# Gated attention and long convolution: the convolution added after the last matmuls, and two of four table groups without their last addition

## The chip, the cores and the metric

The kernel runs on one core of a Trainium2 chip. The metric is the device time of one execution in microseconds, from its first to its last instruction with what lies around them. The core has four engines that compute here: TensorE (PE, matmuls into the PSUM banks; "PEld" is its weight loading), VectorE (DVE), ScalarE (ACT) and GpSimd (POOL, nearly unused). SyncE (SP) issues all DMAs. Each works through its own list of instructions in order and waits on semaphores.

## The reference, cut to what matters

Input x has 2048 tokens of 512 channels. Two branches read it, and a gate for each token mixes them.

```python
g = sigmoid((x * gate_w).sum(-1, keepdims=True))
# a: attention of 32 heads of 16, in 4 segments of 512 tokens, with a compressive memory
for s in range(4):
    p = softmax(qs @ ks.T * 0.25 + causal_mask)
    a_dot = p @ vs
    a_mem = (phi(qs) @ M) / (phi(qs) @ z + 1e-6)
    o = gh * a_mem + (1 - gh) * a_dot
    M, z = M + phi(ks).T @ vs, z + phi(ks).sum()
a = concat(o) @ wo
# b: one causal convolution over 2048 tokens for each channel
K = real(sum_n C[d,n] * exp(dt[d] * A[d,n] * l) * dt[d] * B[d,n])
b = irfft(rfft(K, 4096) * rfft(x, 4096))[:2048] + x * Dskip
out = g * a + (1 - g) * b
```

Everything is stored as bf16, and the output is bf16 as well.

## The kernel before, in words

A small scheduler class records operations (`op`, `evac`, `dma`) with what they read and write. The string `ORDER` (line 366) then lists every operation by its number: the order on each engine, SP's DMA queue included, follows from it. A trailing `a` or `v` says whether ACT or DVE does an operation that either can do (evacuations and copies, `evac`, line 224; such an operation shows up as line 226 or 229 on ACT and 227 or 230 on DVE). The numbers behind a slash are the buffers or PSUM banks. `replay` and `emit` turn that into five instruction lists with semaphore waits. Nearly every matmul goes through the helper in line 683.

The stages, interleaved by that order:

- *Preparation* (`ssm_prep`, `ssm_powers`, `ssm_cb`, lines 738 to 845): decay factors and their repeated squares, on ACT and DVE.
- *Attention* (`project`, `seg_tokens`, `seg_state`, `scores`, `ophase`), for 4 segments times 4 groups of 8 heads. `scores` makes five score tiles for each, 80 in all. Each tile fills the same four PSUM banks, and ACT takes its exponential (line 1063, 128x2048), so a score tile can be computed only when the exponential before it has been taken. Products of probabilities and values follow, then a normalisation on DVE (lines 1035 to 1038), and a transpose of the head outputs (`ophase`).
- *Tables* (`tables(c)`, lines 1131 to 1215), for 4 groups `c` of 128 channels. The convolution kernel K at lag l is a sum over 128 states. The lags are written as sums of an exponent in `F_EXP` (20) and one in `G_EXP` (32). DVE fills a table F and a table G of complex powers, doubling them: `cmul` (line 1149) multiplies entries by a power of the decay in three instructions, a product with one part (line 1159, into the table), a product with the other part (line 1162, into a buffer t2), and their addition (line 1166). G's entries 16 to 23 and 24 to 31 are two calls of eight entries each, instructions of 128x2048. There is one F and one G buffer and there are two t2 buffers.
- *Table sums* in the same function: for each of 32 positions four matmuls of 64 weight columns by 40 columns, in pairs on the left and right half of the columns, accumulate over real and imaginary parts. Four positions are one operation. The results are evacuated and sent by DMA into the tile KTT, which the transform stage reads.
- *Transforms* (`x_level1`, `tail`, lines 851 and 1219): a transform of x through DRAM (`scr_Z`), and, for two channel halves "a" and "b" of 16 steps each, matmuls, a product on DVE, matmuls back, and a last stage (`fir`). The convolution goes to DRAM (`scr_C`, four stores for each half) and is loaded again into four tiles CTT by segment, eight loads on SP, each waiting for the four stores of its half.
- *Final* (`final(s, tb)`, line 1309), for 16 blocks of 128 tokens: a PSUM bank gets an identity matmul of the convolution (512 columns), four matmuls of x with the diagonal skip (128 columns each) and four of the attention output with wo (512 columns each). ACT or DVE scales the result by 1-g (the attention output already carries g/(1-g)) and SP sends it out. In segment 3 the last of the four matmuls is an operation of its own, since the last heads' output comes late.

Of the kernel before, what the change touches and what calls it, by code (L numbers as in the profile page):

```python
# [348 lines left out]
def c_pe(mode, *ns):  # L349
    return ("P", mode, ns)  # L350
# [17 lines left out]
1225/0 1243/0/0 1231/3/1 1233/5 27a 1/0 34/13 32/4 33/9 17/0 35 36 37 46/11 15/0 1241/1 38/5 174/0 41/4 179/7 12/0 59v/0  # L368
45/13 13/4 47/0 49/1 23/0 57a 201/2/1/1 48 19/0 42 60/3 1244a 62/2 43 44 51/6 61 63v/4 72/2 75v/5 74/6 21/0 73 50/4 54/0
64 202a 84/2 1234a 86/1 18 16 85 87v/2 76 193/0 203 99v/6 52/13 96/2 204/0/0 1242a 589/0 98/2 378/0 97 100 53 28/4/0  # L370
211/7 29a 175/2 108/3 109/1 65 101 205a 294/5/0/2 110 176/0 122/5 77 123v/3 295a 209/1 111v/0 3/0 1232a 180/0 197/4
251/2/2/0 1246/1 213/3 215/0/0/1 120/2 121 88 252a 256/2/1/0 177/1 210a 1245/0 89 212a 1235 182/2 590/1 198/0 178 135v/8
257 591 220/0/1 800/0 221 132/1 66/3 134/6 136 199/0 990v/0 253 258 214v 67/2 133 207/1 222 989v 144/3 137 68 254/2/1
216 112 113 259 208v 2/0 218 145/1 146 5/0 993v/0 159v/7 158/3 997 992v 241/0/3 255a 998/0 242 160 991v 200/0 999
1257/2/1 994 243 1259/1 1260a 80/0 1258a 229/0/2 230 124 78/1 338/1/2 156/3 1247/2/0 1249/3 231 995/1 157 224/0/0 1003
225 339a 379/1 217 161 1261 996 1007/0 1004/1 147v/9 1005 79 219/0/0 380 1000 1248a 223/1 1001/1 1006 125 801/2 1250a
148 1226/3/1 1002 802 226 168v/1 1010/1 237/0/1 238 90/1 1009 91/5 227 1228/2 1008 1227a 239 1251 228 297/3/0 298a 382/0
1011 169 272/0/0 592 170 273 92 296 1262/3/0 1012 232 233/1 1229a 1230 149 236/2 240 244 245 1015 274 1263a 234 263/0/2
264 246/0 260 1013/1 247 102/1 1264/3 235/1 265 1016/0 104/6 1265a 248 103 114/1 267/0/1 268 1266 381 266/1 1014 261/0
1252/2/1 1017 1254/3 1021 269 1236/0/0 115/7 280/0/2 281 1255a 270 271 1238/3 275 1018 1253a 282 116 1019/0 126/1 1020  # L380
1024 276/4 277 1237a 1028/1 1027 249/2 250a/0 278/1 1267/1 1029 284/0/3 285 286 335/0/1/0 593 1025/0 803 987/0 336a
308/0/1 1256 309 279/0 1026 1239a 283 287 1283/1/1 1031/1 1285/2 310 1030 4/0 1286a 288 289/2 304/0/3 1284a 1022/0 305
384/1/2/1 290 1032 340/2/1/1 306 385a 1023 321/0/2 322 1287 341 1037/1/0 1041/3 1038 128/1 1039 1042 127 342 1033/2 323
140/3 1034 1035 313/0/0 1040a 1043a 343 291 314 183 307/1 311 312 386 1050v/0 1036a 315 1052v/0 1049v 1288/0 1048v 1056
196 1057/1 1051v 1275/2/1 1058 117v/4 337 138/1 1240 1062 1046/0 69v/6 1063/1 1273/3 1274a 1276a 325/0/3 326 327 316
1054/0 1289/2/0 317/0 1053 1064 387/3/0 388a 1055 347/0/1 318 1069/1 348 395/0/0 1059 1290a 319/0 1065 299/1/0/0 1066/0
139 349 1067 1074 320/2 324 1277 1045 328 1075/0 300 1291/3 356/0/2 70 129v/5 1292a 329 302 152/4 330/1 331 392 357 396a
1299/0/1 1301/3 81v/7 358 130 1068 1076 301 105v/0 1300a 150/3 1302a 332 351/0/3 352 399/0 292/3 444/1/1 353 93v/3 82
1293 445a 368/0/0 151 1060/0 1077 369 1280/1/0 1070 350/2 354 400a 355 1303 293a 359 1268/0/1 131 370 1278/3 1281a 1279a
106 364/0/1 165v/2 1078/1 1079 365 366 1061 1071 1269a 1270/3 1271a 71 1086 393/1 83 406/0/3 407 1282 1087/0 363/0 367  # L390
1044 166 1088 1272 408 360/3 448/0 361 1072/1 362/1 1296/2/0 394a 333/3 1073 94 334a 95 371 372 373/4 410/0/0 167 411
1047 1080 1090/0 1297a 1294/1 1089 153v/8 397/2 141v/1 374 412 423/0/2 1091 375 154 424 1081/0 1304/3/1 398a 303/0 344
1295a 107 409/1 1306/2 118 1083 425 1298 427/0/3 428 1307a 1305a 1308 164/5 413 1322/0 1084/1 376/2 441/3/1/0 429 345
442a 415/0/1 1085 119 1082 155 416 1100/3/0 1101 1092/0 1093 377a 1094 1309/1 262 443 1096/2 1097 1098 414 391/1 142
162/2 163 383/0 181 417 346 171v/9 1107v/0 1099a 1310/0 1311/2 473/0/0 474 1111v/0 1110v 1113/0 1109v 1108v 1115 422/2
426 418 1116/1 1095a 1102a 1112 419/0 1114 1324/0 1117 542/3/2 420 430 431 1323/1 475 1105 1104 543a 1325/0/2 1326a 1118
# [232 lines left out]

# [794 lines left out]
```

## Time and profile before

| | us |
|---|---|
| median of 3 runs | 312.86 |
| lowest and highest | 312.16, 313.46 |
| the profiled execution, whole | 313.44 |
| the profiled execution, span | 311.6 |
| PE busy | 267.4 |
| DVE busy | 262.9 |
| ACT busy | 270.0 |
| mean granted TensorE clock | 0.965 of full speed |

Busy time is time in which at least one instruction of the engine runs. Matmuls overlap one another, and so do neighbouring instructions on DVE and ACT a little; a mean duration in a row is therefore longer than the step from one to the next. In a row of the timeline stand the start and the time covered, the engine, the line, what it writes and reads, how many instructions are merged, and in brackets the idle time before with what ended it. A row of stretches has, for each engine, busy us and in brackets the number of instructions that touch the stretch, and then the granted clock, the DMA engines' share and GB/s.

### The profile page before, as it was taken

The numbers are of one execution on the slowest core, as the hardware profiler recorded it, in microseconds if no ns is written. First come the engines' busy times: TensorE is split into PE (matmuls) and PEld (weight loads), VectorE is DVE, ScalarE is ACT, GpSimd is POOL, SyncE is SP. The second block draws the span as 40 slices with busy tenths as digits, with TensorE's granted clock in tenths as the row PEclk, the third lists the DMA queues.
The fourth block names the chain that finished last, engine by engine and source line by source line (L and its number), as shares of the span: only waits on it lengthen the run. The fifth ranks groups of instructions, "written<-read, shape, count | busy, mean of one in ns | idle before, by whom it ended". The sixth has DMA issues, their size and how long they took to land.

```text
span 311.6 us, 9347 instructions
## 1 busy us (share of the span) xinstructions
PE 267.4 (86%) x3868; PEld 175.6 (56%) x3868; DVE 262.9 (84%) x638; ACT 270.0 (87%) x323; POOL 3.2 (1%) x9
## 2 busy tenths in 40 slices
PE   1787687698778899899988999999999999879991
PEld 1442354364444666586765576767767667555550
DVE  1999899989999989998999998989994999883440
ACT  2898998999999999989999989999899999985221
POOL 2000000000000000000000000000000000000000
PEclk9997995989998999999999999999999999998999
DMA  5999423151333754656665578787688784466141
GB/s 138 237 230 207 106 87 107 40 143 41 95 91 88 202 142 116 176 166 181 176 189 152 172 202 253 218 238 209 197 251 240 209 253 113 131 177 201 50 135 52
DMA packets 62362, 49.94 MB, mean 160 GB/s; under 512 B 23920, under 2 KB 57712, under 8 KB 62320
## 3 DMA queue, kind: packets, MB, share of 16 engines
q1 hardware_dynamic: 62320, 49.35, 56.7%
q8 instruction: 30, 0.49, 0.7%
q14 instruction: 12, 0.10, 0.1%
HBM read 29.02 MB, written 8.39 MB: 120 GB/s over the span
## 4 chain that ended last, share of the span: by engine, by line
PE 41%; ACT 35%; DVE 9%; DMA 7%; issue 4%; SPq 3%; DVEq 0%; ACTq 0%
PE psum L683 40%; ACT sb L1063 20%; ACT sb L226 12%; SPq L222 3%; DMA sb<-sb 2%; DVE sb L227 1%; DMA sb<-scr_Z 1%; DMA scr_C<-sb 1%; ACT sb L799 1%; DMA sb<-c_ident 1%; ACT sb L941 1%; DVE sb L1271 1%; ACT sb L992 1%; DMA sb<-c_negm 1%; DVE sb L1162 1%
## 5 line engine op out<-in xcount | busy, mean ns | idle before, releaser
L683 PE MATMUL psum<-sb 128*128 128x17 bf16 (+11 forms) x3780 | 261.2, 235 | 30.2 <-ACT sb L1063 17.6
L683 PEld LDWEIGHTS psum<-sb 128*128 128x128 bf16 (+3 forms) x3780 | 168.8, 99 | 119.3 <-ACT sb L1063 33.9
L1063 ACT ACTIVATE sb<-psum 128x2048 bf16<-128x2048 f32 x80 | 152.1, 1901 | 6.6 <-PE psum L683 6.4
L226 ACT ACTIVATE sb<-psum 128x512 bf16<-128x512 f32 (+3 forms) x171 | 100.3, 647 | 7.2 <-PE psum L683 6.4
L227 DVE CAST sb<-psum 128x512 bf16<-128x512 f32 (+1 forms) x52 | 35.3, 692 | 11.7 <-PE psum L683 10.0
L1159 DVE TENSOR_TENSOR sb<-sb 128x512 bf16<-128x512 bf16 (+3 forms) x52 | 34.0, 659 | 0.1
L1166 DVE TENSOR_TENSOR sb<-sb 128x512 bf16<-128x512 bf16 (+3 forms) x52 | 33.8, 661 | 0.1
L1162 DVE TENSOR_TENSOR sb<-sb 128x512 bf16<-128x512 bf16 (+3 forms) x52 | 33.7, 659 | 0.1
L1271 DVE TENSOR_TENSOR sb<-sb 128x1024 bf16<-128x1024 bf16 x32 | 21.8, 682 | 2.4 <-ACT sb L226 1.3
L1075 DVE TENSOR_TENSOR sb<-sb 128x1024 bf16<-128x1024 bf16 (+1 forms) x40 | 22.7, 576 | 1.0 <-ACT sb L1063 0.9
L229 ACT ACTIVATE sb<-psum,sb 128x512 bf16<-128x512 f32 x8 | 5.4, 686 | 14.9 <-PE psum L683 14.9
L1038 DVE TENSOR_TENSOR sb<-psum,sb 128x256 bf16<-128x256 f32 x32 | 13.3, 418 | 0.3
L230 DVE TENSOR_SCALAR sb<-psum,sb 128x512 bf16<-128x512 f32 x8 | 5.9, 747 | 6.9 <-PE psum L683 6.9
L1035 DVE RECIPROCAL sb<-psum 128x16 f32<-128x16 f32 x32 | 8.0, 251 | 4.2 <-PE psum L683 4.2
L799 ACT ACTIVATE sb<-sb 128x512 f32<-128x512 f32 x18 | 11.3, 643 | 0.0
L1115 DVE TENSOR_TENSOR sb<-psum,sb 128x512 bf16<-128x512 f32 x12 | 8.3, 688 | 0.2
L800 DVE TENSOR_TENSOR sb<-sb 128x256 f32<-128x256 f32 x18 | 7.5, 419 | 1.1 <-ACT sb L799 1.1
L747 PE MATMUL psum<-sb 128*128 128x128 bf16 x24 | 2.7, 280 | 6.4 <-DMA sb<-c_ident 6.3
L808 DVE CAST sb<-sb 128x512 bf16<-128x512 f32 x20 | 8.2, 420 | 0.0
L992 ACT ACTIVATE sb<-sb 128x512 bf16<-128x512 bf16 x12 | 7.6, 631 | 0.0
L801 DVE SCALAR_TENSOR_TENSOR sb<-sb 128x256 f32<-128x256 f32 x18 | 7.5, 419 | 0.0
L941 ACT ACTIVATE sb<-psum 128x512 bf16<-128x512 bf16 x12 | 7.3, 609 | 0.2 <-PE psum L938 0.2
(61 smaller groups left out, 92.4 us busy)
## 6 DMA issues: line engine op xcount, KB each, us to landing
sb<-c_DNM SPq DMA_DIRECT2D x32, 320.0 KB, 3.8
sb<-c_DNM SPq DMA_DIRECT2D x32, 192.0 KB, 3.0
sb<-sb SPq DMA_DIRECT2D x84, 64.0 KB, 2.9
scr_Z<-sb SPq DMA_DIRECT2D x16, 256.0 KB, 2.3
sb<-scr_Z SPq DMA_DIRECT2D x32, 128.0 KB, 3.3
sb<-sb SPq DMA_DIRECT2D x32, 128.0 KB
sb<-in_A_x_dram SPq DMA_DIRECT2D x5, 512.0 KB, 4.5
scr_C<-sb SPq DMA_DIRECT2D x8, 256.0 KB, 3.4
```

The costliest lines, as they stand in the source:

```text
L226: fa = lambda e: e.activation(dst(), src(), ACT.Copy)
L227: fd = lambda e: e.tensor_copy(dst(), src())
L683: mm = lambda e, o_, l, r_, st, sp, **kw: e.matmul(o_, lhsT=l, rhs=r_, start=st, stop=sp, skip_group_check=True, **kw)
L799: op("ACT", ("As", 512), lambda e, sq=sq, Z=Z: e.activation(ap(sq, n=512), ap(Z, n=512), ACT.Square), r=[Z], w=[sq], key=PW[h] + PWS * k)
L992: op("ACT", ("Asx", 512), lambda e: e.activation(ap(eq, n=512), ap(qT, n=512), ACT.Exp), r=[qT], w=[eq])
L1038: op("DVE", ("V1", 256), lambda e: e.tensor_tensor(ap(o1, gi * 16, [[128, 4], [32, 4], [1, 16]]), ap(T, dims=[[68, 4], [17, 4], [1, 16]]), ...
L1063: o = op("ACT", ("Ax", 2048), lambda e, P=P, pT=pT: e.activation(ap(pT, n=2048), ap(P, n=2048), ACT.Exp, scale=0.25), r=[P], w=[pT])
L1075: op("DVE", ("V2", 128 * nb), lambda e, pT=pT, dims=dims: e.tensor_tensor(ap(pT, dims=dims + [[1, 128]]), ap(pT, dims=dims + [[1, 128]]), ...
L1159: op("DVE", ("V2" if n > 1 else "V1", 256 * n), lambda e: e.tensor_tensor(run(tile, ne, dst, 1), run(tile, ne, src, sstep), ap(pw, cl * 51 ...
L1162: op("DVE", ("V2" if n > 1 else "V1", 256 * n), lambda e: e.tensor_tensor(run(t2, n, 0, 1), run(tile, ne, src, sstep), ap(pw, cl * 512 + 2 ...
L1166: op("DVE", ("V2" if n > 1 else "V1", 256 * n), lambda e: e.tensor_tensor(D_(), D_(), ap(t2, n * 128, [[-n * 128, 2], [2 * n, 64], [1, 2 * ...
L1271: op("DVE", ("V2", 1024), lambda e, Y=Y, XAB=XAB, K3=K3: e.tensor_tensor(ap(Y, dims=[[512, 2], [1, 512]]), ap(XAB, dims=[[512, 2], [1, 512 ...
```

## The change

- In `final` the identity matmul goes. A new operation scales the convolution's block by 1-g in place (ACT or DVE; the new order gives 12 to ACT and 4 to DVE), and the last evacuation becomes one DVE instruction: PSUM times 1-g plus the scaled convolution. The matmuls no longer wait for the convolution's loads; the addition does.
- In `tables` G's entries 16 to 31 become one call of 16 entries (128x4096), moved behind F's last two calls. For `c` 0 and 1 (`NTW = 2`) its addition is left out: table and t2 keep the two products, and the sums over positions get four more matmuls each, with t2 as weights of 32 columns, into the lower 32 of each 64 partitions. For `c` 2 and 3 the addition stays. The t2 pool becomes one buffer of twice the size.
- The order is a new one, listing 1827 operations where there were 1825. The order of the 80 exponentials stays. Of evacuations and copies that either engine can do, 34 go from ACT to DVE and 26 from DVE to ACT, the finals not counted. On SP, the load of the causal mask comes earlier, and the load of one half of the convolution for segment 3 comes behind two output stores.

The diff, the list of operations cut to its first and last lines:

```diff
--- before
+++ after
@@ -361,98 +361,100 @@
 PW, PWS = (1.0, 8.0), 0.6
 CB0 = (5.0, 12.0)
 NPM = 8
+NTW = 2
 
 
 ORDER = """
-8/2 22/0 190/0 191 192 194/0 206/1 195 9/4 14/0 0/0 11/1 30/0 10/0 55/1 24/3/1 25v 31/3 26/6/2 6/0 58/2 39/10 40/12 56/4
...
-1776/4/4 1790 1811v 1823a 1812 1780v 1824 1781 1817/6/2 1818 1813/0/3 1777v 1778 1819a 1820 1814 1815a 1816
+14/0 30/0 206/1 8/1 9/4 0/0 24/2/1 25v 31/5 10/0 11/5 26/5/2 38/8 34/9 55/1 58/7 39/0 35 27a 32/1 21/0 36 56/2 37 41/10
...
+1812a 1815 1817a 1819 1820 1816 1821 1767a 1784/3/5 1765 1766 1785 1786 1772/4/0 1773 1774 1768/7/1 1769 1770 1796/6/3
 """
@@ -620,7 +622,7 @@
     T0 = a
     FP = mkpool("F", 10240, 1)
     GP = mkpool("G", 16384, 1)
-    t2P = mkpool("t2", 4096, 2)
+    t2P = mkpool("t2", 8192, 1)
     pwP = mkpool("pw", 2048, NPW)
     kexP = mkpool("kex", 2560, 1)
     TEND = a
@@ -1146,7 +1148,7 @@
                 res.append(dct[e_])
             return res
 
-        def cmul(tile, dct, ne, dst, src, sstep, n, k):
+        def cmul(tile, dct, ne, dst, src, sstep, n, k, add=True):
             pw = pws[(k, h)]
             S.key = k0 + TT * 0.8 * nstep[0] / 50
             S.tag = "tab%d.%d" % (c, nstep[1])
@@ -1159,9 +1161,14 @@
             op("DVE", ("V2" if n > 1 else "V1", 256 * n), lambda e: e.tensor_tensor(run(tile, ne, dst, 1), run(tile, ne, src, sstep),
                                                                  ap(pw, cl * 512, [[2, 128], [0, n], [1, 2]]), ALU.mult),
                r=rd + [pw], w=wr + [tile])
-            op("DVE", ("V2" if n > 1 else "V1", 256 * n), lambda e: e.tensor_tensor(run(t2, n, 0, 1), run(tile, ne, src, sstep),
+            m2 = op("DVE", ("V2" if n > 1 else "V1", 256 * n), lambda e: e.tensor_tensor(run(t2, n, 0, 1), run(tile, ne, src, sstep),
                                                                  ap(pw, cl * 512 + 256, [[2, 128], [0, n], [1, 2]]), ALU.mult),
                r=rd + [pw], w=[t2])
+            if n == 16:
+                m2.deps += prods
+            prods.append(m2)
+            if not add:
+                return t2
             D_ = lambda: ap(tile, 2 * dst, [[ne * 128, 2], [2 * ne, 64], [1, 2 * n]])
             op("DVE", ("V2" if n > 1 else "V1", 256 * n), lambda e: e.tensor_tensor(
                 D_(), D_(), ap(t2, n * 128, [[-n * 128, 2], [2 * n, 64], [1, 2 * n]]), ALU.add), r=[t2], w=wr)
@@ -1169,6 +1176,7 @@
         gm = lambda *a_: cmul(G, gp, NG, *a_)
         k0 = S.key
         nstep = [0, 0]
+        prods = []
         S.tag = "tabc%d" % c
         for e_, k_ in ((0, 0), (4, 1), (5, 2), (7, 3)):
             S.evac(lambda e_=e_: ap(F, 2 * e_, [[FPL, 2], [2 * NF, 64], [1, 2]]),
@@ -1185,10 +1193,10 @@
         gm(8, 0, 1, 8, 6)
         fm(8, 4, 1, 4, 8)
         fm(12, 5, 2, 4, 9)
-        gm(16, 0, 1, 8, 7)
-        gm(24, 8, 1, 8, 7)
         fm(16, 13, 2, 2, 9)
         fm(18, 16, 1, 2, 9)
+        two = c < NTW
+        t2 = gm(16, 0, 1, 16, 7, not two)
         fr = [fp[i] for i in range(NF)]
         gr = [gp[i] for i in range(NG)]
         kex = Tile(kexP, BF16)
@@ -1204,9 +1212,15 @@
                             for A in range(2):
                                 pr = 32 * A + sl
                                 i = mm(e, ap(P, (sl - q0) * 2 * NF, n=2 * NF, p0=64 * A, np_=64), ap(G, (1 - cc) * GPL + pr * 2 * NG, n=2 * NG),
-                                       ap(F, cc * FPL + pr * 2 * NF, n=2 * NF), cc == 0, cc == 1, tile_position=(0, 64 * A))
+                                       ap(F, cc * FPL + pr * 2 * NF, n=2 * NF), cc == 0, cc == 1 and not two, tile_position=(0, 64 * A))
+                        for cc in range(2 if two else 0):
+                            for A in range(2):
+                                pr = 32 * A + sl
+                                i = mm(e, ap(P, (sl - q0) * 2 * NF, n=2 * NF, p0=64 * A + 32, np_=32), ap(t2, cc * 2048 + pr * 32, n=32),
+                                       ap(F, cc * FPL + pr * 2 * NF, n=2 * NF), False, cc == 1, tile_position=(0, 64 * A + 32))
                     return i
-                op("PE", ("P", "C2", (40,) * 16, 240, 320, 16), f, r=fr + gr + [F, G], pw=[P], acq=[kex])
+                nm = 32 if two else 16
+                op("PE", ("P", "C2", (40,) * nm, 15 * nm, 20 * nm, nm), f, r=fr + gr + [F, G] + ([t2] if two else []), pw=[P], acq=[kex])
             S.evac(lambda q0=q0, ns=ns: ap(kex, q0, [[640, 2], [32, NF], [1, ns]]), lambda P=P, ns=ns: ap(P, dims=[[1, 2], [2, NF], [2 * NF, ns]]),
                    40 * ns, r=[P], pw=[kex])
         for A in range(2):
@@ -1314,20 +1328,23 @@
 
         def att(e, hg, last):
             return mm(e, ap(P, n=512), ap(oTT[0], hg * 2048 + t0, n=128), ap(woT, hg * 512, n=512), False, last)
+        sc = lambda: ap(omgT, 4 * s + tb, n=1)
+        ct = lambda: ap(CTT[s], tb * 512, n=512)
+        pe = CTT[s].part()
+        S.evac(ct, ct, 512, r=[omgT, Cp[(s, 0)], Cp[(s, 1)]], pw=[pe], scale=sc, sb=True)
 
         def f(e):
-            mm(e, ap(P, n=512), ap(ident, n=128), ap(CTT[s], tb * 512, n=512), True, False)
             for k in range(4):
-                i = mm(e, ap(P, k * 128, n=128), ap(xTT[0], k * 2048 + t0, n=128), ap(diagT, k * 128, n=128), False, False)
+                i = mm(e, ap(P, k * 128, n=128), ap(xTT[0], k * 2048 + t0, n=128), ap(diagT, k * 128, n=128), k == 0, False)
             for hg in range(3 if s == 3 else 4):
                 i = att(e, hg, hg == 3)
             return i
-        ns = [512] + [128] * 4 + [512] * (3 if s == 3 else 4)
-        o = op("PE", c_pe("F", *ns), f, r=[ident, Cp[(s, 0)], Cp[(s, 1)], xTT[s], diagT, woT] + [oTp[(s, hg)] for hg in range(3 if s == 3 else 4)], w=[P], acq=[ou])
+        ns = [128] * 4 + [512] * (3 if s == 3 else 4)
+        o = op("PE", c_pe("F", *ns), f, r=[xTT[s], diagT, woT] + [oTp[(s, hg)] for hg in range(3 if s == 3 else 4)], w=[P], acq=[ou])
         if s == 3:
             o.deps.append(last_score[0])
             op("PE", c_pe("F", 512), lambda e: att(e, 3, True), r=[woT, oTp[(s, 3)]], pw=[P])
-        S.evac(lambda: ap(ou, n=512), lambda: ap(P, n=512), 512, r=[P, omgT], w=[ou], scale=lambda: ap(omgT, 4 * s + tb, n=1))
+        op("DVE", ("V1", 512), lambda e: e.scalar_tensor_tensor(ap(ou, n=512), ap(P, n=512), sc(), ct(), ALU.mult, ALU.add), r=[P, omgT, pe], w=[ou])
         S.dma(lambda: bass.AP(out, t0 * 512, [[512, 128], [1, 512]]), lambda: ap(ou, n=512), 131072, r=[ou])
 
     S.key = 0.0
```

More of the change, by code (lines that the diff above doesn't have):

```diff
@@ L371 @@
[L371 to L375, printed above, removed]
@@ L456 @@
+1758/0 1762 1806 1793 1526 1788/7/1 1780/6/5 1776/4/2 985/5 1808/0/0 1799a 1787v 1789 1790 1823/7/1 986v 1824 1794 1801
+1775a 1809 1802 1777 1778 1779a 1818/1/2 1781 1807a 1771a 1782 1813/4/3 1814 1763a 1810 1822v 1825 1811 1826 1764/2/4
+1812a 1815 1817a 1819 1820 1816 1821 1767a 1784/3/5 1765 1766 1785 1786 1772/4/0 1773 1774 1768/7/1 1769 1770 1796/6/3
+1797 1798
 """
```

167 lines of the change are left out of this document (85 added, 82 removed).

## The prediction

> **What bounds the kernel now.** I read the page first, then busy time by stretches, then the timeline of the end.
>
> ```profile
> span 311.6 us, 9347 instructions
> PE 267.4 (86%) x3868; PEld 175.6 (56%) x3868; DVE 262.9 (84%) x638; ACT 270.0 (87%) x323; POOL 3.2 (1%) x9
> ```
>
> Three engines are all near 86%, so an average decides nothing. The stretches do (busy us of PE, weight loader, DVE, ACT, POOL, then clock and DMA):
>
> ```profile
> 27.00:62.00 35.00, 26.40 (x360) 14.35 (x358) 33.42 (x85) 33.46 (x43) 0.00 (x0) 0.84 0.39 109
> 62.00:72.00 10.00, 8.89 (x215) 5.89 (x214) 8.77 (x29) 9.73 (x13) 0.00 (x0) 0.87 0.40 111
> 72.00:98.00 26.00, 21.33 (x284) 11.61 (x286) 25.66 (x64) 25.74 (x30) 0.65 (x1) 0.93 0.27 82
> 98.00:109.00 11.00, 9.59 (x249) 6.60 (x250) 10.70 (x35) 10.36 (x14) 0.00 (x0) 1.00 0.61 172
> 109.00:129.00 20.00, 18.57 (x238) 12.27 (x235) 18.54 (x36) 19.85 (x24) 0.00 (x0) 1.00 0.51 143
> 129.00:264.00 135.00, 129.74 (x1970) 93.23 (x1968) 122.27 (x282) 127.58 (x145) 0.67 (x1) 1.00 0.69 200
> 264.00:286.00 22.00, 18.53 (x270) 12.13 (x271) 15.85 (x38) 18.42 (x16) 0.00 (x0) 0.92 0.60 173
> 286.00:306.00 20.00, 19.16 (x176) 11.00 (x173) 7.49 (x15) 4.96 (x8) 0.00 (x0) 1.00 0.30 99
> ```
>
> From 27 to 129 us the first five rows give ACT 99.1 of 102 us and DVE 97.1; PE has 84.8, so some 17 us of room. From 129 to 264 PE is first (129.7 of 135). From 286 on PE alone runs. The last exponential and what follows:
>
> ```profile
> 279.00 26.16 PE L683 MATMUL psum<-sb 128*128 128x128 bf16 x256 [0.54 <-DVE sb L1038]
> 283.80 1.88 ACT L1063 ACTIVATE sb<-psum 128x2048 bf16<-128x2048 f32 x1 [1.78 <-PE psum L683]
> 302.58 0.75 DVE L230 TENSOR_SCALAR sb<-psum,sb 128x512 bf16<-128x512 f32 x1 [1.21 <-PE psum L683]
> 303.89 0.69 ACT L229 ACTIVATE sb<-psum,sb 128x512 bf16<-128x512 f32 x1 [1.93 <-PE psum L683]
> 305.20 0.69 ACT L229 ACTIVATE sb<-psum,sb 128x512 bf16<-128x512 f32 x1 [0.62 <-PE psum L683]
> ```
>
> The last evacuations come every 1.31 us, each waiting for PE. A final sum is 512 + 4x128 + 4x512 = 3072 columns, so a column takes 0.427 ns and the identity matmul of 512 columns 0.218 us. From the last exponential's end (285.68) to the last evacuation's (305.89) are 20.2 us.
>
> **The change part by part.** Positions are read out of the two order lists; prices are rows.
>
> *Final sums.* PE loses 16 identity matmuls. Behind the last exponential the new order has 13 finals of 2560 columns (1.09 us) beside probability sums and a transpose (1.2 us); the first waits for that exponential's banks. Last sum at 285.68+15.4, its addition 0.95 more: 16.1 us with small waits, so **-4.1** (13 x 0.218 = 2.8; the rest is 1.3 us of finals placed ahead). That holds if DVE keeps up:
>
> ```profile
> L1115 DVE TENSOR_TENSOR sb<-psum,sb 128x512 bf16<-128x512 f32 x12 | 8.3, 688 | 0.2
> L230 DVE TENSOR_SCALAR sb<-psum,sb 128x512 bf16<-128x512 f32 x8 | 5.9, 747 | 6.9 <-PE psum L683 6.9
> L993 DVE TENSOR_SCALAR sb<-sb 128x512 bf16<-128x512 bf16 x12 | 3.4, 284 | 0.0
> L992 ACT ACTIVATE sb<-sb 128x512 bf16<-128x512 bf16 x12 | 7.6, 631 | 0.0
> sb<-scr_C SPq DMA_DIRECT2D x8, 256.0 KB, 4.7
> ```
>
> The multiply-add from PSUM is not in the trace; it lies between the first two rows, 0.69 to 0.75. DVE then has 16 x 0.72 + 4 scalings x 0.28 + a mask, one normalisation and an evacuation (2.3): 14.9 us, under PE's by about one. ACT's 12 scalings (0.63 each, 7.6 us) start where it was idle. Each addition needs its scaling, that its load. On SP the load for segment 3, half a, stands behind the outputs of two finals: issued about 3.6 us after the last exponential, landing 4.7 later at 8.3, while DVE comes to that final at 8.1. So it hides, barely; bounds of this term -2 to -5.
>
> *Table entries on DVE.*
>
> ```profile
> L1162 DVE TENSOR_TENSOR sb<-sb 128x2048 bf16<-128x2048 bf16 x12 | 14.5, 1210 | 0.0
> L1162 DVE TENSOR_TENSOR sb<-sb 128x1024 bf16<-128x1024 bf16 x12 | 8.2, 687 | 0.0
> ```
>
> 24 products and additions of 2048 (29.0 us) become 10 of 4096. One costs 1.21 + 2 x 0.52 = 2.26 by the slope of these rows, at most 2.42: 22.6 us, so -6.4 on DVE. ACT is ahead of DVE in those stretches, so I count nothing for it directly; the order spends it on net eight evacuations moved from ACT to DVE. The product buffer is now single and, in groups 0 and 1, held until PE has summed; the next group's first product waits for that, as its copies into the F table did before.
>
> *More sums on PE.* Each of 32 positions of groups 0 and 1 gets four matmuls of 32 weight columns behind four of 64.
>
> ```profile
> 65.23:67.37 2.14, 2.14 (x130) 2.10 (x129) 1.89 (x6) 2.14 (x3) 0.00 (x0) 1.00 0.73 260
> L683 PE MATMUL psum<-sb 128*64 128x40 bf16 x128 | 2.2, 187 | 0.0
> 65.10:65.23 0.13, 0.13 (x4) 0.03 (x1) 0.00 (x0) 0.13 (x1) 0.00 (x0) 1.00 0.57 94
> 67.00:67.10 0.10, 0.10 (x18) 0.10 (x14) 0.10 (x2) 0.10 (x1) 0.00 (x0) 1.00 0.64 225
> 67.26:67.36 0.10, 0.10 (x12) 0.08 (x6) 0.03 (x1) 0.10 (x1) 0.00 (x0) 1.00 0.24 82
> 103.74:103.84 0.10, 0.10 (x12) 0.07 (x6) 0.10 (x1) 0.10 (x1) 0.00 (x0) 1.00 1.17 435
> ```
>
> A group's 128 sums take 2.14 us, one per 16.7 ns; as many again is 2.1 us a group, nothing beside PE's room. But look at the edges. At 187 ns each, 11 or 12 are under way at any time; a window of 0.1 us inside the group touches 18, so six start in it. The window just after the last (rows 5, and 6 for group 1) touches 12: none starts. Before the first, the weight loader works 0.03 of 0.13 us. Going from 128 weight columns to 64 or back costs PE about 0.1 us. The new code goes from 64 to 32 and back at every position: 128 changes. No row shows 64 against 32, so bounds are 0 and 0.1 each; I take 0.1, the nearest row being the same kind of change. [...]
>
> A position then takes 8 x 0.0167 + 2 x 0.083 = 0.30 us, a sum instruction group of four positions 1.2 us where it was 0.27. Where these lie:
>
> ```profile
> 65.34 1.88 ACT L1063 ACTIVATE sb<-psum 128x2048 bf16<-128x2048 f32 x1
> 68.35 1.89 ACT L1063 ACTIVATE sb<-psum 128x2048 bf16<-128x2048 f32 x1
> 67.48 0.70 DVE L227 COPY sb<-sb 128x256 bf16<-128x256 bf16 x4 [0.19 <-PE psum L683]
> ```
>
> Scores and exponentials share four banks, so what PE does between two score groups delays the next exponential once it exceeds ACT's work (3.0 us here). In the new order five such groups stand between two score groups, then three, in both channel groups. First: 6.0 + 0.5 of others, 1.4 for scores and their mask: next exponential after 7.9 us, against 4.5 were changes free (five at 0.53) and 3.7 of ACT work: 3.4 lost. Then 3.6 + 1.2: 4.8 against ACT's 3.05: 1.75. In channel group 1: 3.5 and 1.9 likewise. Sum **+10.5** (0 to 12). DVE's next table waits too (third row: it waited already) and gets as late as ACT, so nothing makes it up: both have under 5% room up to 129 us.
>
> *The order.*
>
> ```profile
> 26.89 1.88 ACT L1063 ACTIVATE sb<-psum 128x2048 bf16<-128x2048 f32 x1 [0.21 <-PE psum L683]
> L226 ACT ACTIVATE sb<-psum 128x512 bf16<-128x512 f32 x157 | 92.3, 649 | 6.6 <-PE psum L683 5.9
> ```
>
> Ahead of the first exponential ACT has 29 operations for 33, four evacuations less at 0.59 (92.3/157) or 2.3 us; the mask's load is moved ahead of the powers' copies on SP, so it is not what is late next: **-2.0** (0 to -2.7). From there to 129 ACT's work falls by 0.5: **-0.5**. From 129 to 264 PE decides and its work is 0.3 less: **-0.3** (+-3: PE idled 5.3 us there; the new order's waits aren't known). Before the last exponential ACT waited 1.78 us, a final standing in front of the scores; now two finals stand there, each shorter than an exponential: **-1.0** (0 to -2).
>
> Sum: -4.1 + 10.5 - 2.0 - 0.5 - 0.3 - 1.0 = **+2.6**. The profiled execution took 313.44 us (1.84 around its span), so 316.0; the median of the runs is 0.58 lower, so 315.5.
>
> **Rivals.**
> - *The change between 64 and 32 columns is free.* PE takes 2.1 us more a group in its room. Then -7.9: 305.0 us. For it: no row has this change. Against: the edges above, with rows unchanged. This is the case on the other side; it decides below some 0.025 us a change.
> - *It costs, but half is made up.* PE had 4.7 us of room from 72 to 98; if ACT and DVE catch up by their own idle time (2.9 and 4.9 us from 27 to 129), about 310.
> - *DVE's lateness adds.* It has 6.7 us of work behind the last product before it needs PE's sums, which now take 11: 4.5 us of stop in each group. If one of these comes on top, or the new order stalls the PE stretch, 320.
>
> **Chances.** Forecast 0.63 (its own range 311 to 320), free change 0.17, made up 0.10, worse 0.10. The range 305 to 320.5 leaves out the better half of the second case and half of the last. A measurement here tells 0.5%, 1.6 us, from nothing. Faster by more: 0.165 of the free case, 0.06 of the third, 0.05 of the forecast: 0.28. Within: 0.18 of the forecast and 0.02: 0.20. Slower: 0.52.
>
> **What would show it.** The sums of groups 0 and 1 taking 9 to 10 us of PE in place of 2.1, with exponentials 8 and 5 us apart there and DVE idle behind PE; groups 2 and 3 at 2.1 as before; finals 1.09 us apart at the end, each addition waiting for PE, and 16 us from the last exponential to the last addition. If the two groups' sums take about 4.5 us each, the forecast is wrong and the time is near 305. If additions at the end wait for ACT or follow each other without a gap, the -4.1 is too large.

## The result and the profile after

The changed kernel takes 324.0 us (median of 4 runs, 321.76 to 324.37), the kernel before 313.16 us beside it (4 runs, 312.16 to 314.61): a ratio of 1.033 with a 95% interval of 1.027 to 1.039. It is slower by about 11 us, where 2.6 were forecast, and the time lies above the range of 305 to 320.5. Where the runs of a kernel fall into a faster and a slower lot, the ratios compare the faster lots alone.

The first rows of the page of the changed kernel, and its row of the granted clock in 40 slices of 8.07 us:

```profile
span 322.6 us, 9789 instructions
PE 279.4 (87%) x4070; PEld 190.8 (59%) x4108; DVE 272.2 (84%) x644; ACT 270.6 (84%) x319; POOL 3.2 (1%) x9
PEclk9997897955699957999999999999999999999999
```

PE is busy 12 us longer than before, though 16 identity matmuls are gone. (38 of the 4108 matmul records are missing in this trace, while the weight loads are all there.) Behind lower slices up to 57 us, which the kernel before has as well, the clock row has two dips: slices 9 to 11, which is 65 to 89 us, and slices 15 and 16. These are the places of the sums of channel groups 0 and 1. Busy time by stretches of the changed kernel shows it sharper (columns as in the prediction: PE, weight loader, DVE, ACT, POOL, clock, DMA):

```profile
63.40:65.30 1.90, 1.90 (x50) 1.51 (x48) 1.58 (x6) 1.90 (x3) 0.00 (x0) 1.00 0.01 3
65.30:86.00 20.70, 20.00 (x297) 12.96 (x298) 10.76 (x33) 10.25 (x15) 0.00 (x0) 0.51 0.09 25
86.00:109.00 23.00, 18.21 (x292) 11.49 (x294) 21.09 (x46) 22.53 (x26) 0.64 (x1) 1.00 0.22 67
109.00:126.80 17.80, 17.36 (x289) 11.54 (x290) 9.21 (x35) 9.11 (x11) 0.00 (x0) 0.71 0.40 114
126.80:144.00 17.20, 16.50 (x244) 11.52 (x245) 16.54 (x42) 16.97 (x21) 0.00 (x0) 1.00 0.50 134
```

In the second and the fourth row DVE and ACT work half of the time, and PE is busy throughout: it is what they wait for. And there its clock is granted at 0.51 and 0.71 of full speed. The kernel before has 1.00 where its own sums run (65.23 to 67.37 us, in the prediction).

What the three engines lose is seen in the exponentials. Timeline of ACT in the changed kernel, channel group 0:

```profile
64.04 1.93 ACT L1065 ACTIVATE sb<-psum 128x2048 bf16<-128x2048 f32 x1
69.54 0.44 ACT L226 ACTIVATE sb<-psum 128x320 bf16<-128x320 f32 x1 [3.58 <-PE psum L685]
...
74.61 1.88 ACT L1065 ACTIVATE sb<-psum 128x2048 bf16<-128x2048 f32 x1 [0.26 <-PE psum L685]
79.49 0.57 ACT L226 ACTIVATE sb<-psum 128x480 bf16<-128x480 f32 x1 [3.01 <-PE psum L685]
...
81.53 1.88 ACT L1065 ACTIVATE sb<-psum 128x2048 bf16<-128x2048 f32 x1 [0.76 <-PE psum L685]
...
85.39 1.88 ACT L1065 ACTIVATE sb<-psum 128x2048 bf16<-128x2048 f32 x1 [0.49 <-PE psum L685]
```

From the first to the second are 10.57 us (7.9 forecast, 3.01 before), to the third 6.92 (4.8 forecast). What ended the idle time in brackets is PE each time.

One operation of four positions, as a stretch at the start of the sums, one of the same kind in the dip, and one of channel group 2, which has no 32-column matmuls:

```profile
63.41:64.71 1.30, 1.30 (x35) 1.02 (x33) 0.99 (x4) 1.30 (x3) 0.00 (x0) 1.00 0.01 3
67.80:69.43 1.63, 1.63 (x37) 1.25 (x33) 0.00 (x0) 0.00 (x0) 0.00 (x0) 0.50 0.04 10
155.22:155.47 0.25, 0.21 (x13) 0.24 (x15) 0.25 (x1) 0.25 (x2) 0.00 (x0) 1.00 1.19 258
```

The price of the sums at full clock is what the prediction says (1.2 forecast, 1.29 from start to start). The clock of 0.50 in the second row is not in it.

The end of the changed kernel (the last exponential, the last two additions, then the groups of the additions and of the scalings), and the long products of the tables:

```profile
298.68 1.87 ACT L1065 ACTIVATE sb<-psum 128x2048 bf16<-128x2048 f32 x1
...
314.99 0.75 DVE L1347 SCALAR_TENSOR_TENSOR sb<-psum,sb 128x512 bf16<-128x512 f32 x1 [0.34 <-PE psum L685]
316.09 0.75 DVE L1347 SCALAR_TENSOR_TENSOR sb<-psum,sb 128x512 bf16<-128x512 f32 x1 [0.34 <-PE psum L685]
L1347 DVE SCALAR_TENSOR_TENSOR sb<-psum,sb 128x512 bf16<-128x512 f32 x16 | 11.4, 743 | 1.3 <-PE psum L685 1.1
L229 ACT ACTIVATE sb<-sb 128x512 bf16<-128x512 bf16 x12 | 7.7, 711 | 2.7 <-DMA sb<-scr_C 2.7
L1161 DVE TENSOR_TENSOR sb<-sb 128x4096 bf16<-128x4096 bf16 x4 | 9.1, 2284 | 0.0
```

From the last exponential's end (300.55) to the last addition's (316.84) are 16.3 us, as forecast, and the last two additions come 1.10 us apart, each waiting for PE. Not every addition does: three of the 16 wait for PE, 1.1 us in all, and behind an evacuation that waited for it (0.62 us) four additions follow one another without a stop. DVE is close behind PE there. So the loss lies in the two channel groups.

### The profile page after: what moved, and what is told of

It is laid out like the page before. It is cut to its first block, busy times and chain, and to the rows that moved or that the text cites. A ratio compares the mean times of both kernels' runs of the same rounds, so it can differ in the third digit from the quotient of the medians.

```text
span 322.6 us, 9789 instructions
## 1 busy us (share of the span) xinstructions
PE 279.4 (87%) x4070; PEld 190.8 (59%) x4108; DVE 272.2 (84%) x644; ACT 270.6 (84%) x319; POOL 3.2 (1%) x9
## 4 chain that ended last, share of the span: by engine, by line
PE 49%; ACT 23%; DVE 15%; issue 5%; DMA 5%; SPq 1%
PE psum L685 48%; ACT sb L1065 15%; ACT sb L226 7%; DVE sb L1173 2%; DVE sb L1164 2%; DVE sb L227 2%; DMA sb<-in_A_x_dram 2%; DVE sb L1285 2%; DVE sb L1161 2%; DMA sb<-c_DNM 1%; DMA sb<-c_ident 1%; DMA sb<-sb 1%; SPq L222 1%; DVE sb L803 1%; DVE sb L802 1%
## 5 line engine op out<-in xcount | busy, mean ns | idle before, releaser
L685 PE MATMUL psum<-sb 128*128 128x17 bf16 (+11 forms) x3982 | 272.5, 234 | 29.9 <-ACT sb L1065 13.8
L685 PEld LDWEIGHTS psum<-sb 128*128 128x128 bf16 (+4 forms) x4020 | 183.5, 100 | 116.3 <-ACT sb L1065 27.3
L226 ACT ACTIVATE sb<-psum 128x512 bf16<-128x512 f32 (+2 forms) x160 | 93.3, 629 | 24.8 <-PE psum L685 21.4
L227 DVE CAST sb<-psum 128x512 bf16<-128x512 f32 (+2 forms) x61 | 41.3, 685 | 13.5 <-PE psum L685 13.2
L1164 DVE TENSOR_TENSOR sb<-sb 128x512 bf16<-128x512 bf16 (+4 forms) x48 | 33.5, 698 | 0.2
L1161 DVE TENSOR_TENSOR sb<-sb 128x512 bf16<-128x512 bf16 (+4 forms) x48 | 33.4, 703 | 0.2
L1173 DVE TENSOR_TENSOR sb<-sb 128x512 bf16<-128x512 bf16 (+4 forms) x46 | 29.3, 637 | 0.5
L1347 DVE SCALAR_TENSOR_TENSOR sb<-psum,sb 128x512 bf16<-128x512 f32 x16 | 11.4, 743 | 1.3 <-PE psum L685 1.1
L801 ACT ACTIVATE sb<-sb 128x512 f32<-128x512 f32 x18 | 11.6, 648 | 0.1
L227 DVE COPY sb<-sb 128x256 bf16<-128x256 bf16 x18 | 4.6, 292 | 7.6 <-PE psum L685 7.6
L944 DVE TENSOR_SCALAR sb<-psum 128x512 bf16<-128x512 bf16 x12 | 5.0, 416 | 6.0 <-ACT sb L943 6.0
L229 ACT ACTIVATE sb<-sb 128x512 bf16<-128x512 bf16 x12 | 7.7, 711 | 2.7 <-DMA sb<-scr_C 2.7
L227 DVE COPY sb<-psum 128x1024 bf16<-128x1024 bf16 x4 | 2.7, 685 | 6.4 <-PE psum L749 6.4
L994 ACT ACTIVATE sb<-sb 128x512 bf16<-128x512 bf16 x12 | 7.6, 635 | 0.0
```

The source lines that it names most:

```text
L226: fa = lambda e: e.activation(dst(), src(), ACT.Copy)
L227: fd = lambda e: e.tensor_copy(dst(), src())
L685: mm = lambda e, o_, l, r_, st, sp, **kw: e.matmul(o_, lhsT=l, rhs=r_, start=st, stop=sp, skip_group_check=True, **kw)
L801: op("ACT", ("As", 512), lambda e, sq=sq, Z=Z: e.activation(ap(sq, n=512), ap(Z, n=512), ACT.Square), r=[Z], w=[sq], key=PW[h] + PWS * k)
L1161: op("DVE", ("V2" if n > 1 else "V1", 256 * n), lambda e: e.tensor_tensor(run(tile, ne, dst, 1), run(tile, ne, src, sstep), ap(pw, cl * 51 ...
L1164: m2 = op("DVE", ("V2" if n > 1 else "V1", 256 * n), lambda e: e.tensor_tensor(run(t2, n, 0, 1), run(tile, ne, src, sstep), ap(pw, cl * 51 ...
```

## The experiments

Theory A: the changes between 64 and 32 weight columns, and what they do to the clock, cost it. Rival B: the new order, or the single product buffer, costs it. Rival C: matmuls of 32 columns are slow in themselves. All kernels start from the changed one; ratios are to the kernel before, run on the same chip, with 95% intervals.

**The additions back on DVE** (`dveadd`). One instruction behind the second long product of groups 0 and 1, and no 32-column matmuls:

```diff
-            if not add:
-                return t2
...
-                        for cc in range(2 if two else 0):
+                        for cc in range(0):
```

> The last additions of channel groups 0 and 1 are back on DVE (one 128x4096 addition behind the second product of each group), PE sums 128 products a group again, order and final sums stay as in the changed kernel. Theory A (PE's sums of two column widths cost the 22 us that the two groups lose in the trace): a sum group of four positions takes 0.27 us again, the granted clock does not fall to 0.50 from 65 to 86 us, and the time is 324.0 - 22.2 = 302 us plus up to 2 x 2.3 us for the additions on DVE: 302 to 307. Theory B (the new order, or the single product buffer that the next group waits for, costs it): 315 us or more, with the exponentials of groups 0 and 1 still 5 to 8 us apart.

Measured: 307.72 us (306.81 to 308.71), ratio 0.988 (0.983 to 0.993). The loss is gone; B falls, since order and buffer are those of the changed kernel. At 16 us under the changed kernel, it lies a little above the 302 to 307 forecast. One thing that was expected did not come: even here the clock was not full in the sums. PE had been busy for 1.61 of the 3.40 us before them, and then the clock fell to 0.50 and stayed there for 6.8 us (65.69 to 72.52):

```profile
61.60:65.00 3.40, 1.61 (x12) 0.52 (x10) 3.37 (x3) 2.55 (x3) 0.00 (x0) 1.00 0.46 154
65.20:67.20 2.00, 1.85 (x65) 1.71 (x66) 2.00 (x9) 1.81 (x2) 0.00 (x0) 0.62 0.00 0
```

**The same matmuls in another order** (`group4`, `group12`). In the operation's function the loop over positions is run twice, first for the 64-column matmuls, then for the 32-column ones; in `group12` the second loop runs in the bank's last operation, over all positions of the bank (its line is shown; `group4` has `range(sl0, sl0 + 4)` there):

```diff
                     for sl in range(sl0, sl0 + 4):
                         for cc in range(2):
...
+                    for sl in (range(q0, q0 + ns) if sl0 == q0 + ns - 4 else ()):
                         for cc in range(2 if two else 0):
```

In both, a later position's start mark stands between a position's first sum and its 32-column products in the same bank. Whether the upper table entries' first sums are still added to there, no run shows. The matmuls are the same, so the times can be read; `banked` below marks only the first position.

> The same 256 matmuls a group with the same operands; inside a group of four positions the 16 of 64 columns come first and then the 16 of 32 columns, so 2 changes of width in place of 8. Theory A: 32 x 16.7 ns + 2 x 0.11 to 0.12 = 0.76 us for four positions (1.29 at full clock and 1.63 at half in the changed kernel), some 6.1 us a group in place of 12.3 and 10.9, little or no half clock; 303 to 309 us. Rival C (a matmul of 32 columns is itself slow, not the change): four positions stay at 1.3 us or above, and the time within 2% of 324. Rival B (order): also near 324, but with the sums at 0.76.

> The 32-column matmuls of all positions of a PSUM bank (12, 12 and 8) stand in the bank's last sum group: 3 banks x 2 changes of width in a channel group in place of 64. Theory A: four positions take 0.27 us, the last of a bank 0.27 + 0.80 + 0.23 = 1.3 us; a channel group 2 x 2.14 + 3 x 0.23 = 5.0 us; no half clock; 302 to 307 us, at or under the kernel with 2 changes in four positions. Rival C: 2.1 + 64 x 0.1 = 8 us or more a channel group and 315 us or more.

Measured: `group4` 305.72 us (304.38 to 306.76), ratio 0.982 (0.976 to 0.987); `group12` 303.95 us (302.39 to 306.37), ratio 0.975 (0.967 to 0.982). Both lie where A put them. Four operations of `group4` as one stretch:

```profile
64.06:66.72 2.66, 2.66 (x131) 2.38 (x129) 2.36 (x8) 2.54 (x3) 0.00 (x0) 1.00 0.03 7
```

That is 0.665 us for four positions at full clock, 0.76 expected. The 256 matmuls of a group are neither more nor fewer than in the changed kernel: the order of the two shapes alone is worth 18 us.

**All with 32 columns** (`all32`). The 64-column products are taken in two halves, 384 matmuls a channel group, no change of width in between:

```diff
+                        for hh in range(2 if two else 0):
+                            for cc in range(2):
+                                for A in range(2):
+                                    pr = 32 * A + sl
+                                    i = mm(e, ap(P, (sl - q0) * 2 * NF, n=2 * NF, p0=64 * A + 32 * hh, np_=32), ap(G, (1 - cc) * GPL + pr * 2 * NG + 32 * hh, n=32),
+                                           ap(F, cc * FPL + pr * 2 * NF, n=2 * NF), cc == 0, cc == 1 and hh == 0, tile_position=(0, 64 * A + 32 * hh))
```

> Every product of groups 0 and 1 is taken with 32 weight columns: the 64-column ones are split in two halves, so four positions have 48 matmuls of 32 columns and no change of width among them. Theory A: 48 x 16.7 ns = 0.80 us for four positions, 6.4 us a channel group, clock at 1.00, 303 to 310 us. Rival C (32-column matmuls or their four places in the array are slow in themselves): more of them than in the changed kernel, so over 1.3 us for four positions and 324 us or more.

Measured: 309.98 us (307.02 to 311.43, 10 runs), ratio 0.993 (0.989 to 0.997). C falls, and more clearly than expected. Four operations as a stretch, and two rows of PE's timeline in this kernel:

```profile
62.47:64.07 1.60, 1.60 (x192) 1.60 (x192) 1.30 (x5) 1.60 (x3) 0.00 (x0) 1.00 0.01 3
66.79 1.73 PE L685 MATMUL psum<-sb 128*32 128x40 bf16 x24 [1.80 <-issue]
104.17 1.53 PE L685 MATMUL psum<-sb 128*32 128x40 bf16 x22 [2.72 <-issue]
```

192 matmuls in 1.60 us are 8.3 ns each here, with four places in the array, half of the 16.7 that was expected from 64-column ones in two places (128 in 2.14 us, in the prediction). But after some 225 of them PE stood still for 1.80 us, and in the other group for 2.72, waiting for nothing that the profile shows, and behind each stop the clock was 0.50 for 3.4 us. Without the 4.5 us of stops alone the time would be 305.5 us, near `group4`; that is an estimate, no run has this kernel without them.

**Four changes in place of eight or two** (`pairs`). As `group4`, with two positions at a time and a single start mark in a bank:

```diff
+                    for sp in range(sl0, sl0 + 4, 2):
+                        for sl in range(sp, sp + 2):
...
+                        for sl in range(sp, sp + 2):
                             for cc in range(2 if two else 0):
```

> Between group4 and the changed kernel: two positions' 64-column matmuls, then their 32-column ones, so 4 changes of width in four positions in place of 2 and 8. At 0.104 us a change (1.29 us with 8 and 0.665 with 2, at full clock: 0.625 / 6) four positions take 0.665 + 0.21 = 0.87 us. Theory A1 (each change costs its drain, and the clock falls only when the sums stream for less than about half of the time): 0.87 us, clock 1.00, a channel group 7.0 us, 306 to 310 us. Theory A2 (any frequent change lowers the clock): 0.50 shows in the sums, four positions at 1.1 us or more, 312 us or more.

Measured: 310.06 us (306.31 to 313.76, 10 runs), ratio 0.985 (0.979 to 0.991). The profiled execution, four operations as a stretch:

```profile
61.91:65.40 3.49, 3.49 (x130) 2.94 (x129) 2.74 (x9) 2.54 (x3) 0.00 (x0) 1.00 0.02 6
```

0.873 us for four positions, as expected. With 1.30, 0.873 and 0.665 us for 8, 4 and 2 changes, a change costs 0.107 and 0.104 us at full clock, evenly; what PE does in that time no trace shows. In the profiled execution (307.14 us) the clock is 1.00 from 32 to 302 us, the sums of both groups included. The ten runs reach from 306.31 us (mean clock 0.991) to 313.76 (0.962); whether the clock fell in the sums where it was lower, or elsewhere, no trace shows.

**All changes kept, more matmuls between them** (`filler`, `filler2`, `filler1`). The first two products of a position are repeated six times, twice or once; each starts the sum anew, so its value stays:

```diff
-                        for cc in range(2):
+                        for cc in [0] * (6 if two else 0) + [0, 1]:
```

> The changed kernel's sums with all 128 changes of width, and in each position of groups 0 and 1 its first two 64-column products repeated six times more (each starts the sum anew, so the sum is the same). A position then streams 20 matmuls in place of 8: 12 x 16 ns more, so 0.324 + 0.19 = 0.52 us and 2.06 us for four positions if the clock stays at 1.00. Theory A1 (a low share of streaming, 8 x 16.7 of 324 ns, lowers the clock, not the change itself): clock 1.00 through the sums, 2.06 us for four positions, the other matmuls there at full speed, a channel group 16.5 us; 326 to 334 us. Theory A2 (the changes lower it): clock 0.50 there, 0.407 + 12 x 32 ns = 0.79 us a position, 3.2 us for four, 25 us a channel group; 340 us or more.

> As filler, with the first two products of each position repeated twice, not six times: 12 matmuls a position, 256 more than the changed kernel in the two groups, all 128 changes of width kept. Theory A1 (the low share of streaming lets the clock fall): clock 1.00 in the sums, a position 0.324 + 4 x 0.016 = 0.39 us, 1.55 us for four. By the gaps of pairs (0.87 us for four positions), five and three such groups between score groups: 2.85 + 5 x 0.68 + 0.69 + 3 x 0.68 = 9.0 us lost in channel group 0 and 2.35 + 3.4 + 1.33 + 2.0 = 9.1 in group 1, where the changed kernel loses 12.4 and 9.9. So more matmuls make it faster: 324.0 - 4.2 = 320 us (318 to 322). Theory A2, or a share still too low: clock 0.50, 0.407 + 4 x 0.032 = 0.535 us a position, 2.1 us for four, 328 us or more.

> One repetition: 10 matmuls a position, 128 more in the two groups. If the clock stays at 1.00: 0.356 us a position, 1.42 us for four, and 16.0 us lost in the two channel groups in place of 22.2, so 318 us (316 to 320). If it falls to 0.50 as in the changed kernel: 0.407 + 0.064 = 0.47 us, 1.9 us for four, 326 us or more. Theory A1 doesn't say on which side 10 matmuls lie, only that the clock and the time go together.

Measured: `filler` 331.19 us (one run); `filler2` 330.76 us (330.04 to 331.67), ratio 1.059 (1.053 to 1.064); `filler1` 326.81 us (326.40 to 329.00), ratio 1.048 (1.041 to 1.055). Stretches of `filler` (three operations), of `filler2` (one at the start, one later) and of `filler1` (the same two):

```profile
62.78:68.94 6.16, 6.16 (x243) 5.33 (x241) 2.61 (x8) 2.55 (x3) 0.00 (x0) 1.00 0.01 4
```

```profile
64.00:65.55 1.55, 1.55 (x50) 1.27 (x49) 1.24 (x5) 1.55 (x3) 0.00 (x0) 1.00 0.01 3
69.56:71.62 2.06, 2.06 (x53) 1.68 (x49) 0.00 (x0) 0.00 (x0) 0.00 (x0) 0.50 0.00 0
```

```profile
62.91:64.33 1.42, 1.42 (x43) 1.15 (x42) 1.12 (x4) 1.42 (x3) 0.00 (x0) 1.00 0.01 3
67.89:69.73 1.84, 1.84 (x44) 1.47 (x41) 0.00 (x0) 0.00 (x0) 0.00 (x0) 0.50 0.00 0
```

In group 0 `filler` came out as A1 said, to 0.01 us in an operation: all changes are kept, and the sums run at full clock. So the change of width in itself didn't lower the clock there (A2 falls). In group 1 the clock is full as well, but for 3.4 us (122.51 to 125.92) behind a stop of PE of 1.3 us, for which the profile shows no cause. `filler2` was expected to be faster than the changed kernel and isn't: with four matmuls more in a position the clock still falls. Yet A1's bargain shows between the two: `filler` has eight matmuls more than `filler2` in each of 64 positions, 512 in all, and takes the same time. What each kernel streams in a position (its matmuls times 16.7 ns, as a share of the position's time at full clock) puts them in order:

| kernel | changes in four positions | four positions at full clock, us | streaming | clock in group 0's sums |
|---|---|---|---|---|
| changed kernel | 8 | 1.29 | 41% | 0.50 after 1.9 us |
| filler1 | 8 | 1.42 | 47% | falls to 0.50 |
| filler2 | 8 | 1.55 | 52% | falls to 0.50 |
| pairs | 4 | 0.873 | 61% | 1.00 in the profiled execution |
| filler | 8 | 2.05 | 65% | 1.00 |
| group4 | 2 | 0.665 | 80% | 1.00 |

The number of changes in a given time puts these kernels in the same order, so the table alone can't say which of the two counts. The traces can. In them the clock is 1.00 or 0.50, and from one change of the clock to the next are 3.41 us or a whole multiple of it (in the changed kernel 3.41, 6.83, 10.24, 17.07, 20.48, 27.31 and 194.56). Count a matmul as streaming for 0.427 ns a column (the prediction's price) from its start on, and matmuls side by side once. In the sums of the changed kernel, `filler1` and `filler2` the clock falls nine times; the 3.41 us ahead of a fall hold 9 to 21 changes, and PE streams in 0.24 to 0.32 of them (in the changed kernel, ahead of 65.31, 113.10 and 123.34 us: 12, 21 and 19 changes, 0.28, 0.25 and 0.26). In the sums of `pairs` and `filler` stretches of that length with 12 to 14 changes stream for 0.38 to 0.42, and the clock stays. And the kernel before, which has no matmul of 32 columns, shows five such falls ahead of its end with not one change of width in the 3.41 us before, at shares of 0.26 to 0.44. One of them:

```profile
57.85:61.26 3.41, 2.37 (x54) 1.77 (x54) 2.95 (x7) 3.41 (x7) 0.00 (x0) 1.00 0.03 5
61.26:64.67 3.41, 3.35 (x20) 1.51 (x20) 3.10 (x6) 3.14 (x5) 0.00 (x0) 0.50 0.43 120
```

So it is the low share of streaming that goes with the falls, not the number of changes. A single threshold isn't shown, and "less than about half", expected for `pairs`, was an estimate: from 0.40 to 0.44 the traces of the kernel before have both a fall and a clock that stays.

**The best version, and PE's part in the end** (`banked`, `fin_id`). `banked` is `group12` with a single start mark in a bank; `fin_id` adds to it an identity matmul of 512 columns in each final, whose product is overwritten:

```diff
-                                       ap(F, cc * FPL + pr * 2 * NF, n=2 * NF), cc == 0, cc == 1 and not two, tile_position=(0, 64 * A))
+                                       ap(F, cc * FPL + pr * 2 * NF, n=2 * NF), cc == 0 and (sl == q0 or not two), cc == 1 and not two, tile_position=(0, 64 * A))
```

```diff
         def f(e):
+            mm(e, ap(P, n=512), ap(ident, n=128), ap(woT, n=512), True, False)
             for k in range(4):
```

> As group12 (32-column matmuls of a whole PSUM bank behind its 64-column ones), with one start mark in a bank (the first position's) in place of one in each position, so that every position's first sum stays and is added to. No instruction more or less, so theory A says the time of group12: 302 to 307 us (304.0 there), 2 to 3.5% under the kernel before. The rival, that group12's low values were chance, says 307 to 311, as with the additions on DVE.

> banked with one 512-column identity matmul more on PE in each of the 16 final sums, ahead of the others; its product is overwritten by the sum's own start, so the output stays. This gives back what PE was spared in the final sums; DVE and ACT keep the additions. Theory (the end is bound by PE alone): 13 finals behind the last exponential x 0.218 us = 2.8 us longer than banked, finals 1.31 us apart again in place of 1.09. Rival (DVE's additions or the scalings' loads set the end): under 1 us longer.

Measured: `banked` 305.16 us (303.64 to 307.02, 6 runs), ratio 0.976 (0.970 to 0.981); `fin_id` 308.04 us (307.15 to 308.55, 6 runs), ratio 0.985 (0.980 to 0.989). `banked` beats both kernels, inside the 302 to 307 us that the order of `group12` let expect. Its page, and its exponentials in group 0:

```profile
span 305.2 us, 9789 instructions
PE 258.6 (85%) x4070; PEld 178.3 (58%) x4108; DVE 271.8 (89%) x644; ACT 269.3 (88%) x319; POOL 3.2 (1%) x9
PEclk9998799899999999999999999999999999999997
```

```profile
64.45 1.93 ACT L1065 ACTIVATE sb<-psum 128x2048 bf16<-128x2048 f32 x1
68.64 1.87 ACT L1065 ACTIVATE sb<-psum 128x2048 bf16<-128x2048 f32 x1
71.56 1.89 ACT L1065 ACTIVATE sb<-psum 128x2048 bf16<-128x2048 f32 x1
...
74.27 1.91 ACT L1065 ACTIVATE sb<-psum 128x2048 bf16<-128x2048 f32 x1
```

4.19, 2.92 and 2.71 us, in place of 10.57, 6.92 and 3.86, and ACT does not wait for PE ahead of them. The identity matmul given back costs 2.9 us, as forecast (2.8). The last exponential and the last two additions of `fin_id`:

```profile
279.92 1.87 ACT L1065 ACTIVATE sb<-psum 128x2048 bf16<-128x2048 f32 x1
...
298.95 0.75 DVE L1349 SCALAR_TENSOR_TENSOR sb<-psum,sb 128x512 bf16<-128x512 f32 x1 [0.56 <-PE psum L685]
300.26 0.75 DVE L1349 SCALAR_TENSOR_TENSOR sb<-psum,sb 128x512 bf16<-128x512 f32 x1 [0.56 <-PE psum L685]
```

They come 1.31 us apart again and wait for PE longer: the end is PE's alone, with the additions on DVE in its shade.

## Why the prediction was off, step by step

*The step that failed* is the term "More sums on PE", +10.5 us with bounds 0 to 12. That a change costs PE time was right, and so was its price: "A position then takes ... 0.30 us, a sum instruction group of four positions 1.2 us"; it took 1.29, and a change 0.104 to 0.107 us where 0.1 was taken. That a change between 64 and 32 columns costs what the row of 128 against 64 shows was an estimate. In the changed kernel's first sums (63.41 to 65.3 us) it is seen: 0.116 us from the last start of a 64-column matmul to the first of a 32-column one, and 0.109 us back. What was not asked is which clock PE would be granted while it does this. The gaps between exponentials show how much that is. ACT's timeline of `pairs` in group 0:

```profile
62.53 1.93 ACT L1065 ACTIVATE sb<-psum 128x2048 bf16<-128x2048 f32 x1
68.39 1.87 ACT L1065 ACTIVATE sb<-psum 128x2048 bf16<-128x2048 f32 x1
72.32 1.88 ACT L1065 ACTIVATE sb<-psum 128x2048 bf16<-128x2048 f32 x1
```

With 0.873 us for four positions the gaps are 5.86 and 3.93 us, with five and three operations between the score tiles. Five operations longer by 0.42 us each, and three, give 7.96 and 5.19 at 1.29 us and full clock, beside a forecast of 7.9 and 4.8. (The same rule gives 11.8 and 7.5 for `filler`; measured were 12.14 and 7.62. In group 1, with the stop and the fall of the clock, it gives 11.5 and 7.9 for 13.20 and 9.34.) The changed kernel had 10.57 and 6.92. In group 1 the gaps of `pairs` are 5.59 and 4.37, so the rule gives 7.69 and 5.63; the changed kernel had 9.06 and 7.09:

```profile
109.24 1.97 ACT L1065 ACTIVATE sb<-psum 128x2048 bf16<-128x2048 f32 x1
118.30 1.88 ACT L1065 ACTIVATE sb<-psum 128x2048 bf16<-128x2048 f32 x1 [0.94 <-PE psum L685]
125.39 1.88 ACT L1065 ACTIVATE sb<-psum 128x2048 bf16<-128x2048 f32 x1 [0.51 <-PE psum L685]
```

So, with all gaps in one sum:

| part of the sums' loss | us |
|---|---|
| changes of width at full clock: the four gaps by the rule, less those of `banked` (4.19, 2.92, 3.92, 3.83) | 11.6 |
| what the four gaps are longer than the rule, the clock at 0.50 in a part of each or all of it | 7.2 |
| clock at 0.50 up to the next exponential (3.86 us, 2.71 in `banked`) | 1.15 |
| sum | 19.9 |
| measured, the changed kernel less `banked` | 18.8 |

The first line is the forecast's term (10.5), the next two, 8.3 us, are what it lacked, and 324.0 - 315.5 = 8.5 us is what the time was off. The split is an estimate: the rule is taken from one execution of `pairs`, and no kernel has the same 256 matmuls in the same order at full clock throughout. The bound of 12 was too low for the same reason: it took 0.1 us as the most that a change can cost, and left out that what lies between changes can take longer too. The half clock also slowed what is not a sum: of the gap from 64.04 to 74.61 us, five operations of 1.29 to 1.63 us explain 7.6, and scores, mask and the others took the rest.

*Final sums, -4.1*: right in size. The working has a slip: 15.4 and 0.95 make 16.35 us, not 16.1; 16.29 were measured. From the last exponential's start to the end of the span are 23.9 us in place of 27.8, and `fin_id` shows that 2.9 of the 3.9 are the identity matmuls. ACT's scalings waited 2.7 us for the convolution's loads (711 ns each, 631 taken), and DVE did not wait for them. The sign named for a miss, additions that follow each other without a gap, was there in part, and the term held all the same.

*Table entries on DVE*: a product of 4096 took 2.28 us (2.26 taken). That nothing was counted for DVE's saving was too careful in one way: `banked` is 2.6 us faster than `dveadd`, which has the additions on DVE. So once the sums are grouped, leaving the addition out is the faster way; how much of the 2.6 is DVE's work isn't shown, since `dveadd` also ran part of its sums at half clock.

*The start, -2.0, and the ACT stretch behind it, -0.5*: the first exponential came 3.1 us earlier in the changed kernel (23.77 us), but by the seventh only 0.6 of it was left, before any of the new sums. In the traces ACT does 27 operations from the first to the seventh for 24 before, 20.94 us for 18.92. What was moved out of ACT's way at the start came back at once. In `banked` the thirty-third exponential comes 0.5 us earlier than before, where the two terms made -2.5; its grouped sums are in that figure too.

*The PE stretch, -0.3, and the waits before the last exponential, -1.0*: -0.7 and -2.4, from the seventy-third exponential on for the latter. These and the other terms without the sums were forecast as -7.9. `banked`, whose sums have 12 changes for 128, is 8.1 us under the kernel before by the medians, and 6.4 by the spans of the profiled executions. That the sum is near is in part luck: by the spans of `banked` the start and the ACT stretch together made -0.5 for -2.5 and the PE stretch +0.3 for -0.3, and the waits before the last exponential made -2.4 for -1.0. The rival "The change between 64 and 32 columns is free", with its 305.0 us, had the right time for a kernel that hardly makes such changes.

*The other rivals*: little was made up. The seventeenth exponential, behind group 0, came 11.1 us later than before and the twenty-third still 9.6; the twenty-sixth, behind group 1, 20.2 and the thirty-third 18.0. "Half is made up" asked for more. "DVE's lateness adds": DVE did wait for PE, 9.7 us from 60 to 90, but ACT waited for the same sums, and nothing is seen on top. From the seventeenth exponential to the twenty-third the changed kernel takes 16.96 us, and so does `banked`, which has the same single product buffer and the same order and whose seventeenth comes 0.3 us earlier than before.

## What to carry to other kernels

Matmuls of different tile widths on PE are to be grouped, a whole PSUM bank or more at a time: each change between 64 and 32 columns cost 0.104 to 0.107 us here at full clock, and the same 32 matmuls took 1.3 us alternating, 1.6 with the clock halved, and 0.67 in two lots. When many short matmuls with stops between them are added, ask for the clock as well as for the stops: read the granted clock stretch by stretch, and take a price at half speed, the lowest clock in these traces (0.50), as the upper bound, for everything that PE does in that place. And work taken out of the way of a stage's start must go somewhere: here 3.1 us won at the first exponential were down to 0.6 by the seventh, where ACT did three operations more and was busy for 20.94 of 22.12 us.

## What had not been expected of the hardware

- The clock was halved while PE was busy 20.00 of 20.70 us by the profile (changed kernel, 65.30 to 86.00 us, mean clock 0.51). The stops in the sums ahead of the fall were short: 0.109 and 0.116 us from one matmul's start to the next, one every 0.16 us. In these traces the clock changed in steps of 3.41 us, and what went with its falls was a low share of streaming: 0.24 to 0.32 of such a step in the sums, while at 0.38 to 0.42 it stayed. A busy PE in the profile does not tell the two apart: in `filler` it was busy 6.16 of 6.16 us at a clock of 1.00.
- The spread of the runs goes with the clock. The 13 runs of the kernel before that `banked` is compared with reach from 310.13 us (mean clock 0.987) to 314.74 (0.960).
- 32-column matmuls in four places of the array took 8.3 ns each (`all32`), 64-column ones in two places 16.7 (the kernel before). In `all32`, behind some 225 such short ones PE stood for 1.8 and 2.7 us, waiting for nothing that the profile shows; whether the supply of instructions is the cause was not tried.
